# Start-up of a fused attention and MLP kernel: how the first two x tiles are loaded, and where the bias is transposed

## The chip, the cores and the metric

The kernel runs on one core of a Trainium2 chip. The metric is the device time of one execution in microseconds (us). The profile's span is about 2 us shorter than that time and starts at its own zero; all moments below are on the clock of the span. Every execution whose state is on record was classed as fast, with a granted TensorE clock of 1.0, or 0.999 in two that are named below; of the six executions of the kernel before in the first comparison the record has only the times.

Some words: a *look* is one profiled execution. psA, psF and psO are areas of PSUM, the memory to which the matmuls of this kernel write; to *evacuate* a result is to copy it from there to SBUF, where the other tiles lie. rstd is one over the standard deviation, by which a row is normalised. K is the key cache of the first head; it is loaded and transposed in two halves.

## The reference, cut to what matters

```python
# x: (1, 2048, 512) bf16; 32 heads of 128; k_cache, v_cache: (1, 32, 2048, 128); w1: (512, 1792), w2: (1792, 512)
xn = _layernorm(x, axis=-1)
s  = attention(xn @ wq, k_cache, v_cache) @ wo        # softmax over 2048 keys, 32 heads
h  = relu(xn @ w1 + b1) ** 2
g  = _silu(h @ w2 + b2)
return x + s * g
```

Before any attention score can be computed, the first rows of x have to be loaded, normalised, transposed and projected with wq, and the first head's K has to be loaded and transposed.

## The kernel before

The program is one long stream per engine with explicit semaphores; `E` puts an instruction on an engine and returns a token that others can wait for. The parts that matter:

```python
def ln_bn(j, i, c0=0, c1=D):              # statistics of an x tile, on DVE
    ...
    t_bn[jt] = E(DV, partial(_bn_stats, ...),
                 deps=[t_xl[jt], t_x0 if jt == 0 else None, t_xn.get(jt - TPB), t_xr.get(jt - TPB)])

def gen_scores(pi):                       # first head: 8 matmuls into one half of psA
    ...
    deps=[t_k0[b], t_q0[qt], t_exp[pi - 2] if pi >= 2 else t_b1[0]]

# loads at the start; AC and SP are the two queues that issue
t_x0    = S.emit_dma(AC, ... x_ln[P // 2:P, 0, :] ...)      # second half of tile 0
t_xl[0] = S.emit_dma(SP, ... x_ln[0:P // 2, 0, :] ...)      # first half of tile 0
ln_load(0, 1, AC)                         # tile 1
load_k0(0)                                # K of head 0, first half, SP
fill_wq(0, AC)                            # projection weights of head 0
load_k0(1)                                # K, second half, SP
...
# order of the start-up work; each engine keeps this order
warm_up(36); k0_transpose(0); k0_copy(0)
ln_bn(0, 0); ln_rstd(0, 0, eng=DV); ln_bn(0, 1); ln_scale(0, 0)
first_transpose(0); k0_transpose(1); bias_rows(); k0_copy(1)
ln_rstd(0, 1, eng=DV); first_copy(0); bias_copy(); first_proj(0)
ln_scale(0, 1); first_evac(0); first_transpose(1); gen_scores(0)
```

`bias_rows` transposes b1 (14 rows of 128) on TensorE into a corner of psA, `bias_copy` copies it to SBUF on VectorE (DVE) and sets the token `t_b1[0]`, for which the first two score tiles wait.

The softmax here doesn't subtract the row's maximum and nothing guards it: scores larger than these inputs give would overflow.

Of the kernel before, what the change touches and what calls it, by code (L numbers as in the profile page):

```python
# [9 lines left out]
P = 128  # L10
# [204 lines left out]
def bass_recurrent_scan__mha_block_cached__dense_activation_squared_relu__prompt_kernel(  # L215
# [19 lines left out]
    TPB = QB // P  # L235
# [16 lines left out]
    S = _Sched()  # L252
    PE = S.eng("PE")
    AC = S.eng("ACT")
    DV = S.eng("DVE")
    GP = S.eng("POOL")
    SP = S.eng("SP")
# [26 lines left out]
    x_ln = sb("x_ln", [P, TPB, D], BF16)  # L284
# [18 lines left out]
    def bankF(i):  # L303
        return psF[:, i * 512:(i + 1) * 512]
# [9 lines left out]
    sl_xl = [S.slot(f"xl{i}") for i in range(TPB)]  # L314
# [24 lines left out]
    t_xl = {}  # L339
    t_xn = {}  # L340
    t_xr = {}
# [3 lines left out]
    def ln_load(j, i, eng=SP):  # L345
        jt = j * TPB + i
        t_xl[jt] = S.emit_dma(
            eng, partial(_dma, out=x_ln[:, i, :], in_=A_x[0, jt * P:(jt + 1) * P, :]), sl_xl[i],
            deps=[t_xn.get(jt - TPB)])
# [3 lines left out]
    def ln_bn(j, i, c0=0, c1=D):  # L353
        jt = j * TPB + i
        k = 6 if c0 else 0
        t_bn[jt] = E(DV, partial(_bn_stats, out=st_t[:, i, k:k + 6], in_=x_ln[:, i, c0:c1]),
                     deps=[t_xl[jt], t_x0 if jt == 0 else None, t_xn.get(jt - TPB),
                           t_xr.get(jt - TPB)])

    def ln_rstd(j, i, n=1, eng=GP):  # L360
        jt = j * TPB + i
# [8 lines left out]
    def ln_stats(j, i):  # L370
        ln_bn(j, i)
        ln_rstd(j, i)

    def ln_scale(j, i):
        jt = j * TPB + i
        t_xn[jt] = E(DV, partial(_ts, out=xn_t[:, i, :], in0=x_ln[:, i, :],
                                 scalar1=mv_t[:, i, 0:1], scalar2=rstd[:, i:i + 1],
                                 op0=ALU.subtract, op1=ALU.mult),
                     deps=[t_xr[jt], t_xnr.get(jt - TPB)])
# [36 lines left out]
    def k0_transpose(b):  # L416
        n = NKT // 2
        for c in range(n):
            t_kT0[b] = E(PE, partial(_peT, out=bankO(b).bitcast(BF16)[:, c * P:(c + 1) * P],
                                     in_=kT[:, NSL - 1, (b * n + c) * P:(b * n + c + 1) * P],  # L420
                                     ident=ident[:]),
                         deps=[t_k0[b], t_ident], inc=(c == n - 1))

    def k0_copy(b):
        n = NKT // 2 * P
        t_k0[b] = E(AC, partial(_act, out=kT[:, 0, b * n:(b + 1) * n],
                                in_=bankO(b).bitcast(BF16), func=ACT.Copy), deps=[t_kT0[b]])

    def first_transpose(i):
        for c in range(NDC):  # L430
            t_xT[i] = E(PE, partial(_peT, out=bankF(1)[:, 0:256].bitcast(BF16)[:, c * P:(c + 1) * P],
                                    in_=xn_t[:, i, c * P:(c + 1) * P], ident=ident[:]),
                        deps=[t_xn[i], t_ident, tok_xT[0][i - 1] if i else None],
                        inc=(c == NDC - 1))
        t_xnr[i] = t_xT[i]

    def first_copy(i):
        tok_xT[0][i] = E(
            DV, partial(_copy, out=xnT[:, :, i * P:(i + 1) * P],
                        in_=bankF(1)[:, 0:256].bitcast(BF16).rearrange("p (c q) -> p c q", q=P)),  # L440
            deps=[t_xT[i]])
# [3 lines left out]
    def bias_rows():  # L445

        t_b1[0] = E(PE, partial(_peT, out=psA[:, 1536:1600].bitcast(BF16)[:, 0:NFC], in_=b1b[:],
                                ident=ident[0:NFC, 0:NFC]), deps=[tok_b1, t_ident])

    def bias_copy():  # L450
        t_b1[0] = E(DV, partial(_copy, out=b1f[:],
                                in_=psA[:, 1536:1600].bitcast(BF16)[:, 0:NFC]), deps=[t_b1[0]])

    def first_proj(i):
        for c in range(NDC):
            t_proj[0] = E(PE, partial(_mm, out=bankF(0)[:, i * P:(i + 1) * P],
                                      lhsT=wq_sb[:, 0, c, :], rhs=xnT[:, c, i * P:(i + 1) * P],
                                      start=(c == 0), stop=(c == NDC - 1)),
                          deps=[t_wqfill[0], tok_xT[0][i], t_q0[i - 1] if i else None],
                          inc=(c == NDC - 1))  # L460

    def first_evac(i):
        t_evac[0] = t_q0[i] = E(DV, partial(_copy, out=qt_sb[:, 0, i * P:(i + 1) * P],
                                in_=bankF(0)[:, i * P:(i + 1) * P]), deps=[t_proj[0]])
# [64 lines left out]
    def gen_scores(pi):  # L529
        g, k = divmod(pi, NPR)  # L530
        s2, i = pi % 2, g % NSL
        assert t_kfill[g] is not None and t_evac[g] is not None
        t = None
        if g == 0:
            qt, b = divmod(pi, 2)
            for c in range(NKT // 2):
                t = E(PE, partial(_mm_shared, out=psA[:, s2 * 1024 + c * P:s2 * 1024 + (c + 1) * P],
                                  lhsT=kT[:, 0, (b * NKT // 2 + c) * P:(b * NKT // 2 + c + 1) * P],
                                  rhs=qt_sb[:, 0, qt * P:(qt + 1) * P], start=True, stop=True),
                      deps=[t_k0[b], t_q0[qt], t_exp[pi - 2] if pi >= 2 else t_b1[0]],  # L540
                      inc=(c == NKT // 2 - 1))
        else:
            for n in range(2):
                tt = 2 * k + n
                t = E(PE, partial(_mm, out=psA[:, s2 * 1024 + n * 512:s2 * 1024 + (n + 1) * 512],
                                  lhsT=kT[:, i, tt * P:(tt + 1) * P], rhs=qt_sb[:, g % NQS, :],
                                  start=True, stop=True),
                      deps=[t_exp[pi - 2] if pi >= 2 else None, t_kfill[g], t_evac[g],
                            t_bankF[0] if pi == 0 else None],
                      inc=(n == 1))  # L550
        if k == NPR - 1:
            t_S_last[g] = t
        t_exp[pi] = E(AC, partial(_act, out=pT[:, pi % NPT, :],
                                  in_=psA[:, s2 * 1024:(s2 + 1) * 1024],
                                  func=ACT.Exp, scale=SM_SCALE),
                      deps=[t, t_PV[pi - NPT] if pi >= NPT else None])
# [64 lines left out]
    events = {}  # L621
    nfin = [0]

    import os
    dbg = os.environ.get("KDBG")

    pending = []

    def at(step, fn):
# [145 lines left out]
    jobs = []  # L775
# [77 lines left out]
    def load_w1(i):  # L853
# [1 line left out]
        tok_w1[i] = S.emit_dma(SP, partial(_dma, out=w1_sb[:, :, cols], in_=w1_view[:, :, cols]),  # L855
                               sl_w1[i])

    sl_x0 = S.slot("x0b")
    t_x0 = S.emit_dma(AC, partial(_dma, out=x_ln[P // 2:P, 0, :], in_=A_x[0, P // 2:P, :]), sl_x0)
    t_xl[0] = S.emit_dma(SP, partial(_dma, out=x_ln[0:P // 2, 0, :], in_=A_x[0, 0:P // 2, :]),  # L860
                         sl_xl[0])
    ln_load(0, 1, AC)
    load_k0(0)
    fill_wq(0, AC)
# [45 lines left out]
    k0_transpose(0)  # L910
    k0_copy(0)
    ln_bn(0, 0)
    ln_rstd(0, 0, eng=DV)
    ln_bn(0, 1)
    ln_scale(0, 0)
    first_transpose(0)
    k0_transpose(1)
    bias_rows()
    k0_copy(1)
    t_kfill[0] = t_k0[1]  # L920
    ln_rstd(0, 1, eng=DV)
    first_copy(0)
    bias_copy()
    first_proj(0)
    ln_scale(0, 1)
    first_evac(0)
    first_transpose(1)
    gen_scores(0)
    ln_bn(0, 2)
# [38 lines left out]
    credit = 1.0  # L968
    end = NPAIR
    for pi in range(NPAIR):  # L970
        g, k = divmod(pi, NPR)
        if pi >= NPR:
            gen_scores(pi)
        credit = 1.0 if pi < NPR else min(credit + left[0] / max(end - pi, 1), 8.0)
        n = 0
        most = 0 if pi < NPR else 3 if k == 2 else 2
        while n < most:
            late = any(p is not None and NPR * p <= pi + 12
                       for p in [cur_proj[0]] + [x[3] for x in jobs[:4]])
            if not (credit >= 1.0 or late):  # L980
                break
            if k == 1 and cur[0] is not None and cur[0][1] == cur[0][0][0] - 1:
                break
            if not fill_one(pi) and not (not jobs and tail_one(pi)):
                break
            credit = max(credit - 1.0, 0.0)
            left[0] -= 1
            n += 1
        if dbg:
            print(pi, n, round(credit, 1), jobs[0][0] if jobs else None, len(pending))  # L990
        if pi >= NPR:
            gen_pv(pi - LAG)
        if k == 0:
            fill_wq(g + 3)
            fill_k(g + 2)
        if k == LAG - 1:
            fill_v(g + 2)
        if k == LAG + 1 and g >= 1:
            gen_oT(g - 1)
        pending.extend(events.pop(pi, []))  # L1000
        if k >= 2:
            for fn in [pending.pop(0) for _ in range(min(2, len(pending)))]:
                fn()
# [45 lines left out]
```

## Time and profile before

| | before |
|---|---|
| time, first three runs | 1238.45, 1239.90, 1241.53 us |
| time of the profiled execution | 1238.15 us |
| tile 0 normalised, start | 5.73 us |
| tile 1 normalised, start | 7.27 us |
| first scores, start on TensorE | 8.05 us |
| last DVE instruction, start | 1234.12 us |

TensorE (PE in the profile) has hardly a gap from 8 us on, so what happens before the first scores moves the whole of the rest. The prediction shows the chain of waits. Two more lines of the timeline of the kernel before (start, length, engine, line, operation, out<-in) show its end: the projected queries are evacuated, and 0.44 us later the scores start.

```profile
7.61 0.29 DVE L179 CAST qt_sb<-psF 128x128 bf16<-128x128 f32 x1
8.05 1.05 PE L157 MATMUL psA<-qt_sb,kT 128*128 128x128 bf16 x16
```

### The profile page before, as it was taken

Reading aid. Unit: us, or ns where it says so; the run is one execution under the profiler, and the core shown is the slowest. Engines: PE = TensorE matmul, PEld = TensorE weight load, DVE = VectorE, ACT = ScalarE, POOL = GpSimd, SP = SyncE. Lnnn points to the kernel's source line nnn. Section 1 sums busy time; section 2 is a strip of 40 time slices with the busy share of each in tenths; the row PEclk is TensorE's granted clock in tenths of the full one; section 3 lists DMA queues with packets and bytes.
Section 4 is the critical chain, followed back from the end, with each engine's and each line's share of the span. In section 5 each row is a group of like instructions: output and inputs, shape, how many; then the busy total and the mean of one; then the engine's idle time right before and its main releaser. Section 6 shows DMA issues by size and latency. Waiting matters only on the chain.

```text
span 1236.3 us, 26936 instructions
## 1 busy us (share of the span) xinstructions
PE 1231.2 (100%) x11885; PEld 818.7 (66%) x11885; DVE 472.5 (38%) x953; ACT 1053.7 (85%) x1044; POOL 31.9 (3%) x73
## 2 busy tenths in 40 slices
PE   9999999999999999999999999999999999999999
PEld 7666666666666666666666666666666666666666
DVE  4453323244435332334444532333344333324333
ACT  7888888888888888888888888888888888888885
POOL 1010000000002000000000200000000000000000
PEclk9999999999999999999999999999999999999999
DMA  9999997777879797878779978788779799878771
GB/s 213 203 243 194 186 178 134 131 143 142 141 151 170 143 160 129 138 140 144 133 133 170 172 138 144 141 148 133 133 145 148 146 154 158 137 134 147 146 123 31
DMA packets 686884, 185.41 MB, mean 150 GB/s; under 512 B 673552, under 2 KB 685584, under 8 KB 686768
## 3 DMA queue, kind: packets, MB, share of 16 engines
q1 hardware_dynamic: 684592, 179.56, 80.8%
q0 software_dynamic: 1424, 3.81, 1.3%
q8 instruction: 94, 1.54, 0.5%
q10 hardware_dynamic: 752, 0.33, 0.1%
q14 instruction: 22, 0.18, 0.1%
HBM read 96.60 MB, written 2.10 MB: 80 GB/s over the span
## 4 chain that ended last, share of the span: by engine, by line
PE 99%; DVE 0%; DMA 0%; ACTq 0%; issue 0%; DVEq 0%
PE psO L157 38%; PE psA L152 36%; PE psF L152 25%; DMA x_ln<-in_A_x_dram 0%; PE psA L157 0%; DVE out_t L165 0%; PE psF L196 0%; DVE tmp_t L175 0%; PE psO L152 0%; DVE st_t L200 0%; DVE xn_t L171 0%; ACTq L208 0%; PE psO L196 0%; DVE xnT L179 0%; DVE b1f L179 0%
## 5 line engine op out<-in xcount | busy, mean ns | idle before, releaser
L161 ACT ACTIVATE pT<-psA 128x1024 bf16<-128x1024 f32 x1024 | 1043.5, 1023 | 163.6 <-PE psA L152 118.3
L157 PEld LDWEIGHTS psO<-v_sb,pT 128*128 128x128 bf16 x8192 | 547.9, 98 | 240.2 <-issue 12.5
L157 PE MATMUL psO<-v_sb,pT 128*128 128x129 bf16 x8192 | 631.2, 220 | 0.0
L152 PE MATMUL psA<-qt_sb,kT 128*128 128x512 bf16 x2032 | 604.4, 379 | 0.0
L179 DVE COPY o_un<-psO 128x258 f32<-128x258 f32 x256 | 97.3, 421 | 399.6 <-PE psO L157 398.9
L152 PE MATMUL psF<-xnT,wq_sb 128*128 128x512 bf16 (+1 forms) x520 | 168.8, 374 | 0.1
L152 PE MATMUL psF<-wo_all,oT 128*128 128x512 bf16 x480 | 163.6, 379 | 0.0
L152 PEld LDWEIGHTS psA<-qt_sb,kT 128*128 128x128 bf16 x2032 | 157.0, 98 | 0.0
L179 DVE CAST qt_sb<-psF 128x512 bf16<-128x512 f32 (+1 forms) x130 | 87.9, 676 | 97.1 <-PE psF L152 97.1
L165 DVE TENSOR_TENSOR o_bf<-o_un,rden 128x512 bf16<-128x512 f32 x128 | 88.6, 692 | 4.6 <-DVE rden L183 0.3
L152 PEld LDWEIGHTS psF<-xnT,wq_sb 128*128 128x128 bf16 x520 | 50.3, 98 | 59.8 <-DVE xnT L179 0.2
L171 DVE TENSOR_SCALAR r_t<-psF,b1f 128x512 bf16<-128x512 f32 x56 | 42.0, 750 | 117.5 <-PE psF L152 117.5
L152 PEld LDWEIGHTS psF<-wo_all,oT 128*128 128x128 bf16 x480 | 46.9, 98 | 56.4
L152 PE MATMUL psF<-xnT,w_sb 128*128 128x512 bf16 x224 | 77.1, 379 | 0.0
L152 PE MATMUL psF<-w_sb,h2T 128*128 128x512 bf16 x224 | 74.1, 379 | 0.0
L152 PEld LDWEIGHTS psF<-w_sb,h2T 128*128 128x128 bf16 x224 | 21.9, 98 | 26.4
L152 PEld LDWEIGHTS psF<-xnT,w_sb 128*128 128x128 bf16 x224 | 21.9, 98 | 26.4
L165 DVE TENSOR_TENSOR z_t<-psF,b2bc 128x512 f32<-128x512 f32 x16 | 11.1, 692 | 67.2 <-PE psF L152 67.2
L165 DVE TENSOR_TENSOR acc<-psF,acc 128x512 f32<-128x512 f32 x28 | 19.3, 688 | 30.0 <-PE psF L152 30.0
L208 POOL DMA_DIRECT2D out_dram<-out_t x12 | 6.7, 555 | 891.0 <-DVE out_t L165 891.0
L165 DVE TENSOR_TENSOR h2T<-r_t 128x512 bf16<-128x512 bf16 x56 | 23.8, 425 | 1.9
L183 DVE RECIPROCAL rden<-o_un 128x4 f32<-128x4 f32 x128 | 22.9, 179 | 4.4
(47 smaller groups left out, 164.3 us busy)
## 6 DMA issues: line engine op xcount, KB each, us to landing
v_sb<-in_A_v_cache_dram SPq DMA_DIRECT2D x127, 512.0 KB, 4.7
wq_sb<-in_A_wq_dram SPq DMA_DIRECT2D x127, 128.0 KB, 3.0
wo_all<-in_A_wo_dram SPq DMA_DIRECT2D x4, 1024.0 KB, 6.3
w_sb<-in_B_w_dram SPq DMA_DIRECT2D x14, 256.0 KB, 4.6
oT<-o_bf SPq DMA_TRANSPOSE x128, 3.9
x_t<-in_A_x_dram POOLq DMA_DIRECT2D x16, 128.0 KB, 3.6
kT<-in_A_k_cache_dram SPq DMA_TRANSPOSE x127, 4.5
x_ln<-in_A_x_dram SPq DMA_DIRECT2D x14, 128.0 KB, 4.2
```

Source lines behind the costliest of these rows:

```text
L152: return e.matmul(out, lhsT, rhs, start=start, stop=stop)
L157: return e.matmul(out, lhsT, rhs, start=start, stop=stop, skip_group_check=True)
L161: return e.activation(out, in_, func, bias=bias, scale=scale)
L165: return e.tensor_tensor(out, in0, in1, op)
L171: return e.tensor_scalar(out, in0, scalar1=scalar1, scalar2=scalar2, op0=op0, op1=op1)
L179: return e.tensor_copy(out, in_)
L183: return e.reciprocal(out, in_)
L208: return e.dma_start(out, in_)
```

## The change

Tile 0 was loaded in two halves of 64 rows, one on each queue, with tile 1 behind the second half. Now tile 0 goes whole on SP and tile 1 whole on ACT. And the bias transpose and its copy, which stood in front of the first projection and of the normalisation of tile 1, are placed behind them.

```diff
-                     deps=[t_xl[jt], t_x0 if jt == 0 else None, t_xn.get(jt - TPB),
-                           t_xr.get(jt - TPB)])
+                     deps=[t_xl[jt], t_xn.get(jt - TPB), t_xr.get(jt - TPB)])
 ...
-    sl_x0 = S.slot("x0b")
-    t_x0 = S.emit_dma(AC, partial(_dma, out=x_ln[P // 2:P, 0, :], in_=A_x[0, P // 2:P, :]), sl_x0)
-    t_xl[0] = S.emit_dma(SP, partial(_dma, out=x_ln[0:P // 2, 0, :], in_=A_x[0, 0:P // 2, :]),
-                         sl_xl[0])
+    ln_load(0, 0, SP)
     ln_load(0, 1, AC)
 ...
     k0_transpose(1)
-    bias_rows()
     k0_copy(1)
 ...
     first_copy(0)
-    bias_copy()
     first_proj(0)
+    bias_rows()
     ln_scale(0, 1)
     first_evac(0)
+    bias_copy()
     first_transpose(1)
```

(Some debug printing on the host was removed too.)

More of the change, by code (lines that the diff above doesn't have):

```diff
@@ L622, in bass_recurrent_scan__mha_block_cached__dense_activation_squared_relu__prompt_kernel @@
     nfin = [0]
-    import os
-    dbg = os.environ.get("KDBG")
     pending = []
@@ L988, in bass_recurrent_scan__mha_block_cached__dense_activation_squared_relu__prompt_kernel @@
             n += 1
-        if dbg:
-            print(pi, n, round(credit, 1), jobs[0][0] if jobs else None, len(pending))
         if pi >= NPR:
```

## The prediction

> **What bounds the kernel now.** I read the page's busy line first, then the chain that ended last, then the start of the timeline.
>
> ```profile
> PE 1231.2 (100%) x11885; PEld 818.7 (66%) x11885; DVE 472.5 (38%) x953; ACT 1053.7 (85%) x1044; POOL 31.9 (3%) x73
> PE 99%; DVE 0%; DMA 0%; ACTq 0%; issue 0%; DVEq 0%
> ```
>
> TensorE (PE) is busy all the time and carries 99% of the chain. The view of busy time by stretch shows where it is not:
>
> ```profile
> 0.00:8.00 8.00, 5.88 (x65) 5.15 (x65) 3.53 (x12) 3.44 (x4) 3.16 (x14) 1.00 0.80 202
> 8.00:17.00 9.00, 8.93 (x152) 8.44 (x150) 5.11 (x15) 7.16 (x9) 2.08 (x5) 1.00 1.11 212
> 100.00:1200.00 1100.00, 1100.00 (x10562) 727.98 (x10560) 411.08 (x821) 951.06 (x943) 19.04 (x40) 1.00 0.82 147
> ```
>
> The second number is PE busy time: 5.88 of the first 8 us, then practically all of every stretch. The matmuls are the same before and after. So the change can move the end only by moving the moment at which PE's unbroken work begins, and every 0.1 us won there should be won at the end. That moment lies near 8 us. How it comes about is in the chain of waits between 0 and 14 us (start, length, what):
>
> ```profile
> 0.73 0.58 ACTq L208
> 1.31 0.04 issue
> 1.35 3.75 DMA x_ln<-in_A_x_dram
> 5.10 0.02 issue
> 5.12 0.69 DVE st_t L200
> 5.81 0.33 DVE xn_t L171
> ...
> 7.18 0.17 DVE b1f L179
> 7.35 0.33 DVE xn_t L171
> 7.68 0.05 issue
> 7.73 0.40 PE psF L196 x4
> 8.12 0.98 PE psA L157 x16
> ```
>
> The chain starts with the load of the **second** x tile: ACT's queue first issues half of tile 0 (0.73 to 1.31), only then tile 1, which lands at 5.10. VectorE (DVE) works in program order, and the statistics of tile 1 stand in front of the normalisation of tile 0, so tile 0 waits for tile 1:
>
> ```profile
> 4.46 0.57 POOL L165 TENSOR_TENSOR rstd<-ve_t,mhalf 128x1 f32<-128x1 f32 x1 [1.75 <-DVE ve_t L171]
> 5.12 0.69 DVE L200 BATCH_NORM_STATS2 st_t<-x_ln 128x6 f32<-128x512 bf16 x1 [0.75 <-DMA x_ln<-in_A_x_dram]
> 5.73 0.40 DVE L171 TENSOR_SCALAR xn_t<-x_ln,mv_t,rstd 128x512 bf16<-128x512 bf16 x1
> ```
>
> rstd of tile 0 is ready at 5.03, DVE stands idle for 0.75 us until 5.12, and tile 0 is normalised at 5.73: 0.70 us after it could have been. Further on, the copy of the bias b1 at 7.18 stands in front of the normalisation of tile 1 (7.27), whose rstd was ready at 7.04 (POOL, 6.49 + 0.55).
>
> **What the Trainium skill says.** (1) "DMA: Bandwidth & Descriptors", Rules for kernel authors: two transfers to disjoint partition halves share the same engines either way, and one transfer of 128 partitions should be used; its section "Issuing engines are not separate DMA queues" adds that a second issuing engine saves only issue time. The trace agrees in part: the half tile costs ACT's queue 0.58 us of issue, during which tile 1 isn't issued; but the two halves together landed 2.2 and 2.4 us after issue. (2) "Perfetto Trace Analysis", DMA Instruction — HWDGE: the row of a DMA in the profile covers the making of its descriptors in a block that the issuing queues share, not the movement of data. The trace fits: the two issues of 64 rows each, side by side, took 0.58 us, while a later issue of 128 rows took 0.43; the issue of tile 1 beside that of K took 0.85. (3) "PSUM — Partial Sum Buffer", Engine vs sequencer instructions: VectorE is strict FIFO and matmuls start in program order. The trace agrees: the 0.70 us above exist only because of that order.
>
> **The change part by part.**
>
> *a. Loads.* It removes one DMA and one wait; tile 0 goes whole on SP (128 KB instead of 64), tile 1 whole and first on ACT. Tile 1 is issued at about 0.73 instead of 1.31. Price: tile 0 now shares the DMA engines with tile 1. In fine stretches of the trace no data moves before 2.0 us, then about 246 GB/s. Before, tile 0 alone (131 kB) needed 131/246 = 0.53 us, ended near 2.55 and was seen by DVE at 3.27, 0.7 us later. After, both tiles (262 kB) need 1.07 us, and DVE sees both at about 2.0 + 1.07 + 0.7 = 3.8. K used some of those bytes before, which now queues behind tile 0, so I take **3.7** (3.5 to 4.0). Tile 0 is then 0.4 us later than now, tile 1 1.4 us earlier.
>
> *b. The DVE and POOL chain from 3.7*, with the spacings of the trace, from start to start. Statistics of tile 0 at 3.70; aggregate +0.73 = 4.43; epsilon +0.21 = 4.64; POOL +0.25 = 4.89, done +0.57 = 5.46. Meanwhile statistics of tile 1, 4.85 to 5.54, without waiting. Normalise tile 0 at **5.50** (before 5.73): 0.23 us won of the 0.70, because tile 0 itself comes later.
>
> *c. The bias.* Now its transpose (one PE instruction, 0.09 us of weight load and 0.18 us of matmul) stands behind the projection, and its copy (0.17 us) behind the evacuation of the projection. From 5.50: transpose of tile 0 +0.45 = 5.95; its copy to xnT +0.44 = 6.39; projection +0.54 = 6.93 (it waits for that copy, not for the bias transpose, now too). For tile 1: aggregate 5.50 + 0.31 = 5.81; epsilon 6.02; POOL 6.26 to 6.81; normalise tile 1 at **6.84** instead of 7.27, 0.43 us won, of which 0.2 is the bias copy's slot. Evacuation of the projection 6.93 + 0.45 = 7.38 to 7.67. Then the bias copy, 7.59 to 7.76.
>
> *d. The first scores.* In the code they wait for the token of the bias copy (the bias rests in the PSUM of the second score tile, but both score tiles wait for it). Before, that copy was long done. After, it is the last of three: transposes of tile 1 at 6.84 + 0.45 = 7.29, finished issuing near 7.6; evacuation done at 7.67; bias copy done at 7.76. With 0.08 us for the signal the scores start at **7.84**; before, their first weight load was at 8.02. So 0.43 won shrinks to about 0.2.
>
> *e. Sum.* About **0.2 us** sooner for PE's unbroken work, 0.02% of 1239.9. Behind it, the loads of tiles 2 and 3 and of V keep their queue and their order; the short waits of PE up to 15 us are loops through DVE that move along. The removed debug lines run on the host and cost the chip nothing.
>
> **The rivals.**
> - *The loads get worse.* If tile 0 lands at 4.0 or later, normalise 0 starts at 5.8 and with the bias copy nothing is won; 0.1 to 0.3 us may be lost. For it: two simultaneous issues of 128 rows may take 0.85 us rather than 0.58, as tile 1 did beside K, which delays the first data. Against it: ACT no longer issues two DMAs in front of the projection's weights. Time: 1240.0 to 1240.2.
> - *K becomes the wait.* K's first half landed at 4.75 (1.36 + 3.4), just before PE's transposes at 4.75; behind a larger tile 0 it may come at 5.0 or 5.2. The transposes of tile 0 stand behind those of K in PE's order, but only from 5.95, so there are 0.6 us of slack. Time unchanged.
> - *The full gain.* If tile 0 still lands at 3.3 because bandwidth isn't the limit there, normalise 0 starts at 5.1 and the gain is 0.5 to 0.6 us. Against it: the rate of 246 GB/s is already near what the stretch around it reaches (150 to 410). Time: 1239.3.
> - *PE isn't moved at all* because something later pins it, such as tiles 2 and 3. Against it: PE idles only some 0.1 us between 8 and 17 us. Time 1239.9.
>
> **Range and chances.** All rivals lie within 0.6 us of each other; the three runs of before spread over 3.1 us (1238.45 to 1241.53). So the spread of the runs sets the range, not the mechanism. I take 1239.7, and for the median of a few runs against one of another few about 1.9 us each way: 1237.8 to 1241.6. Two per cent are 25 us, more than three times the whole first 8 us that this touches can be shortened or lengthened by such edits, so "same" is all but sure.
>
> **What would show it right or wrong.** In the changed kernel's timeline: (1) statistics of tile 0 start at 3.5 to 4.0, later than 3.27; those of tile 1 follow on the epsilon step with no wait for a DMA. (2) Normalise 0 near 5.5, normalise 1 near 6.84. (3) The bias copy stands right before the first scores, and these start within 0.1 us of its end, near 7.84. (4) From there PE is unbroken as before, and the busy times of sections beyond 17 us are the same. The prediction would be wrong if tile 0 landed as early as now or after 4.2, if the projection's weights or K became the wait, or if the time moved by more than 2 us, which nothing in this start-up could explain.

## The result, and the profile after

| | before | after |
|---|---|---|
| median | 1239.53 us (6 runs, 1238.36 to 1241.53) | 1238.08 us (6 runs, 1237.73 to 1238.59) |
| first scores | 8.05 us | 7.96 us |
| last DVE instruction | 1234.12 us | 1234.03 us |

The ratio of the fast runs is 0.9988, with a 95% interval of 0.9975 to 1.0001. (A ratio here is the mean time of one kernel's fast runs over that of the other's of the same rounds, so not quite the ratio of the medians.) By that interval the two kernels can't be told apart at this level. The medians lie 1.45 us apart, but the two traces only 0.09 us.

The timeline of the changed kernel:

```profile
3.71 0.69 DVE L200 BATCH_NORM_STATS2 st_t<-x_ln 128x6 f32<-128x512 bf16 x1 [3.71 <-DMA x_ln<-in_A_x_dram]
4.72 0.68 DVE L200 BATCH_NORM_STATS2 st_t<-x_ln 128x6 f32<-128x512 bf16 x1
5.24 0.94 PE L196 MATMUL psO<-ident,kT 128*128 128x128 bf16 x8 [0.24 <-DMA kT<-in_A_k_cache_dram]
5.50 0.41 DVE L171 TENSOR_SCALAR xn_t<-x_ln,mv_t,rstd 128x512 bf16<-128x512 bf16 x1
6.03 0.39 PE L196 MATMUL psF<-ident,xn_t 128*128 128x128 bf16 x4
7.44 0.29 DVE L179 CAST qt_sb<-psF 128x128 bf16<-128x128 f32 x1 [0.17 <-PE psF L152]
7.65 0.16 DVE L179 CAST b1f<-psA 128x14 f32<-128x14 bf16 x1
7.96 1.05 PE L157 MATMUL psA<-qt_sb,kT 128*128 128x128 bf16 x16
```

Statistics of tile 0 wait for the load until 3.71 (before: 3.27), those of tile 1 follow at 4.72 with no wait in brackets (before: 5.12, after a wait of 0.75), tile 0 is normalised at 5.50 (before: 5.73). TensorE now waits for K in front of its first transposes (the bracket at 5.24), and the bias copy sits between the evacuation and the scores.

The chain of waits of the changed kernel (start, length, what) runs in this look through the load of K, no longer through that of the second x tile, and shows how long TensorE was held:

```profile
1.18 4.02 DMA kT<-in_A_k_cache_dram
5.20 0.05 issue
5.24 0.94 PE psO L196 x8
6.19 0.24 PE psF L196 x4
```

Beyond the start-up nothing changed. The view of busy time by stretch of the changed kernel (after the length: busy PE, weight loads, DVE, ACT, POOL, then the granted clock, the DMA share and GB/s):

```profile
0.00:8.00 8.00, 6.50 (x66) 5.83 (x67) 3.66 (x12) 3.26 (x4) 3.16 (x14) 1.00 0.82 215
100.00:1200.00 1100.00, 1100.00 (x10562) 727.57 (x10560) 411.38 (x821) 951.02 (x943) 19.04 (x40) 1.00 0.82 148
```

PE is busy for 6.50 of the first 8 us instead of 5.88. Most of that is no gain: the warm-up matmuls and K's transposes ran slower in this look (36 warm-up matmuls in 4.02 us instead of 3.65, 8 transposes in 0.94 instead of 0.62), at a granted clock of 1.00 in both. That is not the change: the 36 took 4.02 us in e1 and e3 too, with the loads of before, and 3.45 in e5 with those of after. From 100 to 1200 us the engines' busy times are those of before to within 0.5 us.

### The profile page after: what moved, and what is told of

It reads as the page before. It is cut to its first block, busy times and chain, and to the rows that moved or that the text cites. A ratio compares the mean times of both kernels' runs of the same rounds, so it can differ in the third digit from the quotient of the medians.

```text
span 1236.3 us, 26934 instructions
## 1 busy us (share of the span) xinstructions
PE 1231.7 (100%) x11885; PEld 818.8 (66%) x11885; DVE 472.8 (38%) x953; ACT 1053.5 (85%) x1044; POOL 31.9 (3%) x73
## 4 chain that ended last, share of the span: by engine, by line
PE 99%; DMA 0%; DVE 0%; issue 0%; SPq 0%; DVEq 0%
PE psO L157 38%; PE psA L152 36%; PE psF L152 25%; DMA kT<-in_A_k_cache_dram 0%; PE psA L157 0%; DVE out_t L165 0%; PE psF L196 0%; DVE tmp_t L175 0%; PE psO L196 0%; PE psO L152 0%; DVE xnT L179 0%; SPq L208 0%; PE psA L196 0%; DVEq L119 0%
```

## The experiments

Eleven runs were made: six new kernels, and repeats of before, of after and of the loads alone. Each was executed five times in turn with the kernel before on the same chip, and profiled once. Rows are by what they do; "first scores" and "last DVE" are the starts of those instructions in the profiled execution.

| run | what it is | first scores | last DVE | median (range), us |
|---|---|---|---|---|
| before | | 8.05 | 1234.12 | 1239.53 (1238.36 to 1241.53) |
| e1_before_again | the same | 8.08 | 1234.14 | 1238.28 (1238.18 to 1238.32) |
| e9_before_third | the same | 8.36 | 1234.42 | 1238.46 (1238.27 to 1238.84) |
| after | | 7.96 | 1234.03 | 1238.08 (1237.73 to 1238.59) |
| e4_after_again | the same | 8.00 | 1234.08 | 1237.95 (1237.67 to 1238.11) |
| e10_after_third | the same | 7.61 | 1233.69 | 1238.03 (1237.72 to 1238.53) |
| e2_loads_only | after, bias in its old place | 7.60 | 1233.66 | 1237.81 (1237.72 to 1238.54) |
| e6_loads_only_again | the same | 7.85 | 1233.92 | 1237.90 (1237.68 to 1238.26) |
| e3_bias_only | before, bias in its new place | 8.44 | 1234.51 | 1238.43 (1238.17 to 1241.63) |
| e5_scores_free | after, first scores don't wait for the bias copy | 7.74 | 1233.81 | 1237.86 (1237.73 to 1238.33) |
| e8_wq_late | after, projection weights issued late | 9.10 | 1235.19 | 1239.25 (1238.81 to 1240.75) |
| e7_needed_order | e5, early loads in needed order on one queue | 7.75 | 1233.83 | 1237.87 (1237.74 to 1238.20) |
| e11_transpose_first | e7, weights sooner, tile 0 transposed before K | 7.83 | 1234.24 | 1238.44 (1238.27 to 1239.28) |

**The gauge.** In every row but the last, "last DVE" minus "first scores" is between 1226.06 and 1226.09 us. So the first scores are a gauge of the end, good to a few hundredths of a us, where the times of a row's executions lie 0.1 to 3.5 us apart. (In e11 the difference is 1226.41; the reason is below.) It tells where one execution stood, not what a kernel takes on average: two looks of after differ by 0.39 us.

### Is the difference of the medians real? (e1, e4, e9, e10)

Theory N says that most of the 1.45 us is scatter; theory L (later L2) says that the kernel before has a start-up that varies and that the change cures it.

> The kernel before, unchanged, as a control. Theory N (the 1.4 us between the medians of before and after are mostly spread between executions; the trace gives 0.09 us): this control is as far from the kernel before as chance makes two equal kernels, so a ratio between 0.9988 and 1.0012, with a spread of 2 to 3 us like before. Theory L (the split load makes the start-up land at a varying time, which the change cures): the control also spreads by 2 to 3 us, and its slower executions have a second x tile that lands later than 5.10 us in a profile.

> The changed kernel again. From the traces 0.09 us sooner than before, ratio 0.9999. Theory N: this time the ratio is nearer to 1 than 0.9988, and the spread is larger than 0.9 us. Theory L: ratio 0.9988 again and a spread under 1 us, and the profile of before on this chip, if it is a slow execution, has a late x tile.

> The kernel before once more, for the tail of slow executions. Theory L2 (before leaves the projection's weights only 0.5 us of slack, landing at 6.63 for a use at 7.16, and some executions overrun it): of this kernel's and the reference runs' executions about one in six is at 1239 us or more. Theory N (the tail has nothing to do with the kernel): as many in the changed kernel as here.

> The changed kernel once more. Theory L2 (its weights are issued 1.1 us sooner, land near 5.4 for a use at 6.9, 1.5 us of slack): none of the five at 1239 or more, median 0.1 to 0.4 us under before. Theory N: ratio 1.0000, executions over 1239 as often as before.

On one chip, e1 had a median of 1238.28 and e4 of 1237.95, 0.33 us apart; on another, e9 had 1238.46 and e10 1238.03, 0.43 us apart. The ratios to the reference runs of before were 0.9999 (0.9986 to 1.0011) and 0.9997 (0.9985 to 1.0010) for the unchanged kernel, and 0.9996 (0.9982 to 1.0009) and 0.9994 (0.9980 to 1.0007) for the changed one. Not one interval leaves 1 outside. Three looks of each give first scores at 8.05, 8.08, 8.36 (mean 8.16) and at 7.96, 8.00, 7.61 (mean 7.86): **0.3 us** sooner. No look of after is later than any of before, but with looks 0.3 to 0.4 us apart within each kernel the size is known only roughly. Traces and these medians agree on 0.3 to 0.4 us, 0.03%. The 1.45 us of the first comparison were mainly scatter: four of its six runs of before took over 1239 us. Of the signs written down for e4, theory N's came half true (the ratio is nearer to 1, but the spread is 0.44 us, not over 0.9), and so did theory L's (the spread, but not the ratio of 0.9988). e10 had no execution of 1239 us or more, as theory L2 expected, and a median 0.43 us under e9's, a little more than the 0.1 to 0.4 expected.

Whether such long executions belong to the kernel before stays open. Of 43 executions of it, 7 took over 1239 us (the one in six of theory L2), of 16 of the changed kernel none. But all 7 are among the 33 reference runs; the 10 that ran as e1 and e9 stayed under 1238.85. Counted afterwards by how x is loaded, 8 of 48 executions with the split tile were that long (one of them in e3), and none of 31 with the whole tile and the queues of after (after, e2, e5, e6). That leans towards L2, but half of the 8 come from one comparison. No long execution of these was profiled, so nothing shows where such a one lost its time. For one of them, of 1240.11 us, the record gives a granted clock of 0.999; 0.1% of the span is 1.2 us (an estimate), so at least there the clock is a rival. What a trace does show is e9: the second tile was seen at 5.43 us instead of 5.12, and the scores started 0.31 us later than in the first look of before. The controls did not have the spread of 2 to 3 us that theory L expected.

### Which part brings it? (e2, e6, e3)

> Only the loads changed, the bias transpose and its copy where they were. Step d of the prediction says the moved bias copy gives back part of the gain: normalise of tile 1 at 7.00 us (after: 6.86) but first scores at 7.80 (after: 7.93, before: 8.02), 0.2 us gained in all. Rival (the bias copy in front of normalise 1 is what costs): scores at 8.0 or later. Theory L: the times are as tight as those of after (under 1 us from lowest to highest) and 0.1 per cent below before. Theory N: the spread and the median may fall anywhere in the range of before.

```diff
 # after, with:
+    bias_rows()            # again in front of k0_copy(1)
     k0_copy(1)
 ...
     first_copy(0)
+    bias_copy()
     first_proj(0)
-    bias_rows()
 ...
-    bias_copy()
```

> Loads changed, bias left in its old place: a second look. Theory W: from the transposes of tile 0 to the first scores 1.86 to 1.90 us again. Theory K (the start of the transposes of tile 0 moves from look to look by when K lands, which now shares the DMA engines with the projection's weights): K's first half lands anywhere from 4.7 to 5.4 us, and the transposes of tile 0 start at the later of normalise 0 + 0.45 and the end of K's transposes. Rival (only x matters): transposes at normalise 0 + 0.45 whatever K does.

(The same kernel.)

> Only the bias moved, tile 0 still loaded in two halves. Step c and d: normalise of tile 1 at 7.07 us instead of 7.27, but the first scores wait for the bias copy and start at 8.05 to 8.12, no sooner than before (8.02). Rival (the bias move is worth its 0.2 us): scores at 7.8. Theory L: spread of 2 to 3 us as before. Theory N: nothing to be told from before.

(The kernel before with the bias lines of after.)

With the loads alone, the first scores start at 7.60 and 7.85, mean 7.73: no later than with both parts (7.86). The 7.80 expected for e2 was missed, because tile 0 was normalised at 5.23 already; so were the 1.86 to 1.90 us of theory W in e6, where it was 2.14, for a reason told below. e6's test of K decides nothing: normalise 0 + 0.45 and the end of K's transposes fell within 0.05 us of each other. With the bias alone the scores start at 8.44, later than in any look of before, and later than the 8.05 to 8.12 expected. Most of that is not the bias: tile 0 was normalised 0.11 us later than in the first look of before (5.84 instead of 5.73) and its transposes took 0.61 us instead of 0.40, so that their copy started 0.31 us later (6.93 instead of 6.62). From that copy to the scores it is 1.51 us instead of 1.43, and these 0.08 us are the bias. The loads bring the gain; the bias move brings none. Why can be read off the end of the start-up. The timeline of the bias-only kernel:

```profile
7.28 0.40 DVE L171 TENSOR_SCALAR xn_t<-x_ln,mv_t,rstd 128x512 bf16<-128x512 bf16 x1
7.92 0.29 DVE L179 CAST qt_sb<-psF 128x128 bf16<-128x128 f32 x1 [0.25 <-PE psF L152]
8.13 0.16 DVE L179 CAST b1f<-psA 128x14 f32<-128x14 bf16 x1
8.44 1.05 PE L157 MATMUL psA<-qt_sb,kT 128*128 128x128 bf16 x16
```

and of the loads-only kernel:

```profile
7.16 0.29 DVE L179 CAST qt_sb<-psF 128x128 bf16<-128x128 f32 x1
7.60 1.05 PE L157 MATMUL psA<-qt_sb,kT 128*128 128x128 bf16 x16
```

From the start of the evacuation to the scores it is 8.44 - 7.92 = 0.52 us where the bias copy stands between them, and 7.60 - 7.16 = 0.44 us where it doesn't. The number is the same in every look: 0.52, once 0.51, in after, e4, e10, e3 and e8; 0.44, once 0.43, in before, e1, e9, e2 and e6. So the moved copy costs 0.08 us. Nor does the bias transpose hold the projection in its old place: from the start of the copy of the transposed tile to the projection it is 0.57 us in before (6.62 to 7.19), in after (6.45 to 7.02) and in e2 (6.17 to 6.74). The earlier normalisation of tile 1 is real (0.35 us behind that copy in e3 and 0.41 in after, instead of 0.65 in before), but the first scores use tile 0 only. In TensorE's order the transposes of tile 1 stand in front of the scores, yet the scores don't wait for them: they start 0.12 us after the evacuation in before and together with it in e5 below, and the 0.44 us are the same.

e6 shows the one thing that speaks for the move: there K's second half was late and pushed the bias transpose to 6.79, and the projection, behind it, started at 6.90, 0.76 us after the copy instead of 0.57. In e5 below, with K as late but the bias moved, it is 0.69 (6.19 to 6.88), so the bias's own share is about 0.07 us by that comparison, and at most the 0.11 us from its start to the projection in e6.

### Is it the token of the bias copy? (e5)

> The changed kernel, but the first score tile no longer waits for the bias copy (only the second one, whose PSUM the bias occupies, does). Theory W (the moved bias copy became the last wait): counted from the start of the transposes of tile 0, the first scores start 1.86 to 1.90 us later (after: 1.93 and 1.94; before: 1.86), so 0.05 to 0.1 us sooner. Rival (the evacuation alone would hold them, the token costs nothing): still 1.93 or 1.94.

```diff
-    deps=[t_k0[b], t_q0[qt], t_exp[pi - 2] if pi >= 2 else t_b1[0]],
+    deps=[t_k0[b], t_q0[qt], t_exp[pi - 2] if pi >= 2 else t_b1[0] if pi else None],
```

The bias rests in the part of psA that the second score tile uses, so the first one is free of it, and the output was correct. The timeline of this kernel:

```profile
7.30 0.29 DVE L179 CAST qt_sb<-psF 128x128 bf16<-128x128 f32 x1 [0.28 <-PE psF L152]
7.51 0.16 DVE L179 CAST b1f<-psA 128x14 f32<-128x14 bf16 x1
7.74 1.05 PE L157 MATMUL psA<-qt_sb,kT 128*128 128x128 bf16 x16
```

It is 0.44 us again, with the bias copy in its new place; e7, with the same freed token, has 0.44 too (7.31 to 7.75). So the 0.08 us are the wait for the token. The number written down as expectation was missed all the same: from the transposes of tile 0 (5.76) to the scores it was 1.98 us, not 1.86 to 1.90, because the projection stood behind K's second transposes, which waited 0.27 us for their load. The gauge of the expectation was too long a stretch; the shorter one, from the evacuation on, tells it.

### What sets the start of the transposes of tile 0? (e4, e8)

In the second look at the changed kernel (e4) the timeline shows:

```profile
5.26 0.41 DVE L171 TENSOR_SCALAR xn_t<-x_ln,mv_t,rstd 128x512 bf16<-128x512 bf16 x1
5.44 0.78 PE L196 MATMUL psO<-ident,kT 128*128 128x128 bf16 x8 [0.44 <-DMA kT<-in_A_k_cache_dram]
6.06 0.39 PE L196 MATMUL psF<-ident,xn_t 128*128 128x128 bf16 x4
```

Tile 0 was normalised at 5.26. In before, the transposes followed 0.46 us later (5.73 to 6.19), which would be 5.72 here; they came at 6.06, because K's transposes stand in front of them, and K was late. K's transposes were slow as well: they held TensorE for 0.62 us (5.44 to 6.06), in e5 and e7 for 0.45 and 0.46; one took 258 ns on the mean in e4 and 220 in those two, with the granted clock at 1.00. At the pace of e5 tile 0 would have waited until 5.89 (an estimate), so about half of the 0.34 us is late K and half slow transposes. Why the pace differs from look to look, no run shows. K's first transposes started at 4.76, 4.82 and 4.84 in the three looks of before, and at 5.24, 5.44 and 4.80 in those of after (in e1 and e10 with no wait for K in the trace, behind the warm-up). Is that the larger tile 0 in front of K, or the projection weights, which ACT now issues at 1.15 instead of 2.23?

> The changed kernel, but the projection's weights are issued about 2.2 us on the ACT queue, as before the change, instead of 1.15. Theory K: K's first half lands 3.3 to 3.6 us after issue (before: 3.4, after: 4.0 to 4.3), so at 4.6 to 4.8, and normalise 0 alone sets the transposes of tile 0 (normalise 0 + 0.45), with scores at 7.6 to 7.8. Rival (K is late because tile 0 in front of it doubled): K lands at 5.2 or later as in the changed kernel.

```diff
-    fill_wq(0, AC)
     load_k0(1)
     E(AC, ... ACT.Exp ...)
+    S.emit_wait(AC, [t_ones])          # POOL's last memset, about 2.1 us
+    fill_wq(0, AC)
```

The timeline of the kernel with late weights:

```profile
4.39 0.61 PE L196 MATMUL psO<-ident,kT 128*128 128x128 bf16 x8
8.15 0.40 PE L152 MATMUL psF<-xnT,wq_sb 128*128 128x128 bf16 x4 [0.73 <-DMA wq_sb<-in_A_wq_dram]
```

K's transposes started at 4.39 with no wait, straight behind the warm-up: with the weights out of the way K is earlier than in any other look, though tile 0 is whole. That half of theory K held, in this one look, and by more than it had said (4.6 to 4.8); and the transposes of tile 0 followed normalise 0 after 0.47 us, as expected. The other half, scores at 7.6 to 7.8, failed: the weights, issued at 2.17 behind both halves of K, took 5.9 us to land (before: 4.4 from an issue at 2.23) and the projection waited for them. The first scores came at 9.10 and the time at 1239.25. So the change did something that the prediction overlooked. In before the weights landed at 2.23 + 4.4 = 6.63 for a projection at 7.19, in after at 1.15 + 4.2 = 5.35 for one at 7.02: their slack grew from about 0.6 to 1.7 us, and K paid for it. e8's runs also spread over 1.94 us, on a chip where e5, e6 and e7 spread over 0.5 to 0.6. That would suit theory L, an arrival on the path bringing scatter, but does not show it: the reference runs of before on that chip spread over 1.79 us, and the longest run of e8 (1240.75) is the other one with a granted clock of 0.999.

### Can the start be made earlier still? (e7, e11)

> All early loads in the order in which they are needed, on one queue: tile 0, tile 1, K, K; the projection's weights on ACT at about 1.9 us; the first scores free of the bias copy. If arrival is what sets the start-up: tile 0 lands so that its statistics start at 3.0 to 3.3, normalise 0 at 4.8 to 5.1, K by 4.6, first scores at 7.2 to 7.4, 0.6 us before the changed kernel, and the time 1237.2 to 1237.5. Rival (one queue can't feed the DMA engines early on, or the weights come too late): scores at 7.7 or later.

```diff
 # e5, with:
-    ln_load(0, 1, AC)
+    ln_load(0, 1, SP)                  # SP: tile 0, tile 1, K, K
     load_k0(0)
-    fill_wq(0, AC)
     load_k0(1)
     E(AC, ... ACT.Exp ...)
+    S.emit_wait(AC, [t_ident])
+    fill_wq(0, AC)                     # issued at 1.91 us
```

```profile
2.91 0.69 DVE L200 BATCH_NORM_STATS2 st_t<-x_ln 128x6 f32<-128x512 bf16 x1 [2.91 <-DMA x_ln<-in_A_x_dram]
4.71 0.41 DVE L171 TENSOR_SCALAR xn_t<-x_ln,mv_t,rstd 128x512 bf16<-128x512 bf16 x1
5.28 0.62 PE L196 MATMUL psO<-ident,kT 128*128 128x128 bf16 x8 [0.28 <-DMA kT<-in_A_k_cache_dram]
5.74 0.39 PE L196 MATMUL psF<-ident,xn_t 128*128 128x128 bf16 x4
7.75 1.05 PE L157 MATMUL psA<-qt_sb,kT 128*128 128x128 bf16 x16
```

Tile 0 was there at 2.91, sooner than hoped, and normalised at 4.71, but its transposes again stood behind those of K, which came at 5.28. K's second half was late too (6.43), and the projection behind it. The expected 7.2 to 7.4 was missed, the rival's 7.7 or later came true, and the scores were no sooner than e5's. So TensorE's order was turned round:

> Tile 0 and tile 1 in order on one queue, the projection's weights at about 1.0 us on the other, TensorE transposes tile 0 before K's first half, the first scores free of the bias copy. If K's place in TensorE's order was what kept the needed-order run at 7.75: transposes of tile 0 at 5.2, projection at 6.1 to 6.3, first scores at 7.1 to 7.4, time 0.3 to 0.5 us under the changed kernel. Rival (the arrival of K and of the weights sets the start, in whatever order): scores at 7.6 or later, or the second score tile waits instead.

```diff
 # e7, with the weights issued at 0.99 us, and on TensorE:
+first_transpose(0); k0_transpose(0); first_proj(0); k0_transpose(1); bias_rows()
-k0_transpose(0); first_transpose(0); k0_transpose(1); first_proj(0); bias_rows()
```

```profile
5.22 0.40 PE L196 MATMUL psF<-ident,xn_t 128*128 128x128 bf16 x4 [0.81 <-DVE xn_t L171]
6.93 0.62 PE L196 MATMUL psO<-ident,kT 128*128 128x128 bf16 x8 [0.32 <-DMA kT<-in_A_k_cache_dram]
7.83 0.61 PE L157 MATMUL psA<-qt_sb,kT 128*128 128x128 bf16 x8
8.67 0.62 PE L157 MATMUL psA<-qt_sb,kT 128*128 128x128 bf16 x8 [0.23 <-ACT kT L161]
```

Now the transposes of tile 0 start at 5.22 and the projection at 6.23, as expected, but K's second half holds the queue of TensorE until 6.93, the scores follow at 7.83 (7.1 to 7.4 had been expected), and the second score tile waits for ACT's copy of K until 8.67. The rival held. That later stop shows in the gauge, 1226.41. By then it is K, and no longer the x tiles, that sets the start.

The best of the kernels by the traces is the loads-only one (7.60 and 7.85), with e5 (7.74) and e7 (7.75) beside it, though one look of after had 7.61. The medians of these runs, 1237.81, 1237.90, 1237.86 and 1237.87, are the lowest of all, but against the kernel before (reference runs of the same jobs: 1238.31 and 1238.48) the intervals, such as 0.9996 (0.9984 to 1.0009) for e5, do not separate them from no difference at all. One rival to the changed loads was not tried: to leave the loads of before and put the statistics of tile 1 behind the normalisation of tile 0 on DVE.

## Why the prediction was right

The measured 1238.08 us lies inside the range of 1237.8 to 1241.6, and "same" came true. The range was made from the scatter of three runs, and the median came to lie 0.3 us above its lower edge: that it holds says little about the mechanism. (The prediction's remark that all rivals lie within 0.6 us of each other is a slip; its own times for them run from 1239.3 to 1240.2.) Step by step:

- **What bounds the kernel** held, and better than it was put: the end follows the first scores to within 0.03 us in twelve of thirteen traces.
- **a, loads.** Statistics of tile 0 were put at 3.7 (3.5 to 4.0); they came at 3.71, 3.47 and 3.40 in three looks. The direction and about the size held, but the 3.71 owes something to luck: two errors cancel. The prediction let 246 GB/s flow from 2.0 us on, though the view of before that it rests on has 67 from 2.0 to 2.2. In after it was still slower at first (51 and 133 GB/s in the two stretches from 2.0 to 2.4, in the first look), then faster: 352 GB/s between 2.6 and 3.0 (351 and 382 in the others), where before moved 187. By 3.0 us 241 kB had moved in the first look, 242 in e4, 266 in e10 (rates times stretches, all loads together), and 246 by the prediction. So the total was right. Yet e4 saw tile 0 0.24 us sooner than the first look with the same total; which tile's bytes went first these views don't tell. The view of busy time by stretch has the rate as its last column; first the kernel before, then the changed one:

```profile
2.60:3.00 0.40, 0.40 (x7) 0.40 (x5) 0.00 (x0) 0.29 (x1) 0.11 (x1) 1.00 1.07 187
```

```profile
2.60:3.00 0.40, 0.40 (x7) 0.40 (x6) 0.00 (x0) 0.39 (x2) 0.11 (x1) 1.00 1.05 352
```

- **b, DVE and POOL chain.** Normalise 0 was put at 5.50 and came at 5.50, 5.26 and 5.20. Each step followed the predicted spacing to a few hundredths; only its start shifts with the landing.
- **c, bias.** Normalise 1 was put at 6.84 and came at 6.86, 6.83 and 6.56. (The 6.83 of e4 is luck: rstd was ready at 6.58, and normalise 1 stood behind the late copy of tile 0.) But that this was a gain of 0.43 us towards the end, which d then shrank, was wrong: the evacuation of tile 0 was the binding step, not tile 1, and no part of that gain could reach the end.
- **d, first scores.** Their first weight load, from which the prediction counted, was put at 7.84 and came at 7.93, 7.96 and 7.58, just before the first matmuls at 7.96, 8.00 and 7.61. That the bias copy becomes the last wait held; e5 shows it, at 0.08 us. In the first look its end came 0.05 us later than predicted (7.81), and the signal took 0.12 us, not 0.08.
- **e, sum.** 0.2 us was predicted; the first two looks give 0.09, three looks each 0.3, the medians of equal jobs 0.33 and 0.43. The size is right, its split between the parts is not: the loads bring all of it, and the bias takes 0.08 back.
- **The rival "K becomes the wait"** was dismissed on "0.6 us of slack". That failed in two looks of three: K's transposes started up to 0.7 us later than in before (5.44 against 4.76), took 0.94 and 0.78 us instead of 0.62, and held tile 0 by 0.07 us in the first look (6.03 instead of 5.50 + 0.46) and by 0.34 us in e4. In the first look the slow transposes alone did it: at the pace of e5 they would have let tile 0 through at 5.69 (an estimate). By the prediction's own signs ("if ... K became the wait") e4 counts against it. Overlooked was that the weights, now issued 1.08 us sooner, share the DMA engines with K (e8).
- **The predicted time** of 1239.7 was 1.6 us too high, nearly all of it in the base. It started from 1239.9, the median of three runs of which two were long; the kernel before settled at 1238.3 to 1238.6 afterwards, and the profiled execution, 1238.15, had already shown that level.

## What to carry to other kernels

Where one engine has no gap after the start-up, take the start of its unbroken work in the trace as the gauge: it tells differences of 0.1 us between executions apart, where medians of five runs could not. But take several looks, because it moved by 0.3 to 0.4 us from look to look of one kernel. Follow every wait into that moment, not just the one the chain names, and give to a moved instruction's token as much thought as to its place: an instruction of 0.16 us that was moved out of the way of tile 1 cost 0.08 us on the path of tile 0. And when loads are issued sooner, ask which other load now shares the engines with them.

## What the Trainium skill lacked or had wrong

- "DMA: Bandwidth & Descriptors", Rules for kernel authors, says of two transfers to disjoint partition halves "Use one 128-partition transfer". The runs agree: halves on two queues let the statistics start at 3.27 to 3.41 us (four looks), one whole tile in front of everything at 2.91 and 2.96 (e7, e11), one whole tile beside another at 3.39 to 3.71 (seven looks). What the row lacks is the cost for the transfer behind: tile 1, issued behind a half at 1.31 us, landed at 5.10.
- "DMA: Bandwidth & Descriptors", Issuing engines are not separate DMA queues, says that all DMAs interleave on the same engines and that issuing on several only saves sequencer time. What it lacks is how far a load issued a little sooner moves the others: weights issued at 1.15 instead of 2.17 us landed 2.7 us sooner (5.35 against 8.07 us, after against e8), and K's first transposes started 0.4 to 1.05 us later (4.80 to 5.44 in three looks of after against 4.39 in e8).
- "Perfetto Trace Analysis", DMA Instruction — HWDGE, has no duration for an issue of few rows. Two issues of 64 rows side by side took 0.58 us each, two of 128 rows side by side 0.40 us each. No page that was found explains why the smaller one takes longer, and no run here does.
